# Three sets of transposes moved from TensorE to DMA in a gated attention and convolution kernel

## The chip, the cores and the metric

The kernel runs on one core of one Trainium2 chip. Times are device microseconds of one execution of the program. The profile is one such execution, with its own time; the other times are of executions without a look inside.

## The reference, cut to what matters

Two branches work on the same x of 2048 tokens by 512 features, and a gate of each token mixes them.

```
g = sigmoid((x * gate_w).sum(-1))
a = attention(x, wq, wk, wv, wo, beta)        # 32 heads of 16, 4 segments of 512 tokens
b = long_convolution(x, A, B, C, log_dt, Dskip)
return g * a + (1 - g) * b

# attention, segment by segment (phi(t) = t + 1 if t > 0 else exp(t)):
for s in range(4):
    a_dot = softmax(qs @ ks.T * scale + mask) @ vs            # causal, inside the segment
    a_mem = (phi(qs) @ M) / (phi(qs) @ z + 1e-6)              # memory of the segments before
    o     = gh * a_mem + (1 - gh) * a_dot                     # gh = sigmoid(beta), by head
    M, z  = M + phi(ks).T @ vs, z + phi(ks).sum()             # state for the next segment
out = o @ wo
```

The convolution's kernel K is a sum over 128 complex exponentials for each feature, and the convolution itself is done by a Fourier transform written as matmuls.

## The kernel before

**How work is ordered.** The kernel is first recorded as a list of operations (`Sched.op`, line 196), each with an engine, an assumed cost, the tiles it reads (`r`), writes (`w`, or `pw` for a part), and a key. `Sched.schedule` (line 268) then plays the list forward with the assumed costs. For each engine it takes the ready operation with the lowest key that could start within 0.12 us of the engine's free time, and appends it. The result is one fixed order for each engine. `Sched.emit` (line 401) writes it out with semaphore waits. On the chip each engine works strictly in that order: an operation that waits holds everything behind it. All loads, stores and copies by DMA go through one queue, SP, in the same way. The planner assumes for a DMA that SP is taken for 0.4 us, that the transfer starts 1.0 us after its issue at the earliest and after the transfer before it, that it takes bytes/215e3 us, and that it lands 1.2 us later (lines 374 to 377).

**Buffers.** Tiles come from pools of a few slots (`ek` and `rk` 2 each, `kT` 3, `o1` and `o2` 2 each, `oT` 5, `xT` 3, `xk` 1, `zs` 2). A tile is given a slot in the planned order, and the first writer waits for the last users of the slot. [...]

**Evacuations.** `S.evac` (line 256) copies PSUM to SBUF on ACT (line 258) or on DVE (line 259), as the planner chooses; line 261 is the ACT form with a scale.

**Stages.**
- Start: parameters of the convolution are loaded, turned by TensorE, and their powers are built on ACT and DVE (`ssm_prep`, `ssm_powers`), until about 60 us.
- Attention, until about 257 us: four segments, each with four head groups `hg` of 8 heads.
  - `do_xT(s)` loads 512 tokens of x by one DMA and turns them by 16 TensorE transposes into `xT[s]` (features on partitions), with two evacuations of 128x1024.
  - `gate_tokens(s)` and `seg_tokens(s)` compute the token gate and the values from `xT[s]`.
  - `project(s, hg)` makes `qT` and `kT`, 128 features by 512 tokens.
  - `seg_state(s, hg)`, for segments 0 to 2: four TensorE transposes turn `kT` to keys by token in PSUM (line 945); ACT takes their exponential (line 948), DVE their maximum with 0 (line 949) and then the minimum of the exponential with 1 (line 950); eight matmuls add phi(k) times v into the state.
  - `group(s, hg, gi)`: score tiles, exponentials of 128x1024 on ACT (line 1038), and weights times values.
  - `ophase(s, hg)`: turns the result to tokens on partitions, divides, and gets the memory part `o2` likewise. Then matmuls with the identity, accumulating over `o1` and `o2`, turn and add them in PSUM (line 1115 inside `f3`), and one evacuation makes `oT` (line 1119).
  - `oproj(s)`: the four `oT` of the segment against `wo`, stored to DRAM.
- Beside the attention run `tables(c)`, four times (DVE, lines 1169 to 1174, then 256 small matmuls and four small DMA copies), and `x_level1` (the first level of the transform of x: 16 steps, each ending in a store to DRAM).
- Tail, from about 240 us: loads of the transform's constants and results, 16 steps `K0` to `K15`, and the final mix, until 388 us.

Matmuls are recorded through the helper of line 717, so most PE work has that line.

Of the kernel before, what the change touches and what calls it, by code (L numbers as in the profile page):

```python
# [7 lines left out]
ACT = mybir.ActivationFunctionType  # L8
BF16 = mybir.dt.bfloat16
# [126 lines left out]
class Sched:  # L136
# [111 lines left out]
        self.ops.append(o)  # L248
        return o

    def dma(self, out, in_, nbytes, r=(), w=(), pw=(), key=None, slow=False, packets=0, issue=0.4):
        kw = {"allow_slow_non_contiguous": True} if slow else {}
        lat = max(nbytes / 215e3, packets * 0.0005)
        return self.op("SP", issue, lambda e: e.dma_start(out(), in_(), **kw), r=r, w=w, pw=pw, key=key, lat=lat)  # L254

# [223 lines left out]
def c_act(n):  # L479
    return 0.17 + 0.000833 * n  # L480
# [6 lines left out]
def c_tt(n):  # L487
    return 0.16 + 0.00052 * n
# [6 lines left out]
def c_ts4(n):  # L495
    return 0.15 + 0.00026 * n
# [78 lines left out]
def build_kernel(nc, A_x, A_wq, A_wk, A_wv, A_wo, A_beta, B_A_re, B_A_im, B_B_re, B_B_im,  # L575
                 B_C_re, B_C_im, B_log_dt, B_Dskip, gate_w, out):
    with contextlib.ExitStack() as es:
        S = Sched(nc, es)
        ap = S.ap
        op = S.op  # L580
        x = A_x[0]
# [17 lines left out]
        ident = cload(np.eye(128), "ident", BF16, -1)  # L599
# [30 lines left out]
        S.addr += 6 * 128  # L630
        omsP = S.pool("oms", S.addr, 512, 2)
        S.addr += 2 * 512
        A0 = S.addr
        a = A0

# [6 lines left out]
        xTP = mkpool("xT", 4096, 3)  # L642
# [16 lines left out]
        oTP = mkpool("oT", 1024, 5)  # L659
# [81 lines left out]
        xT = []  # L741

        def do_xT(s):
            S.tag = "xT"
            xks = Tile(xkP, BF16)
            S.dma(lambda: ap(xks, dims=[[512, 4], [1, 512]]),
                  lambda: bass.AP(x.tensor, x.offset + s * 4 * 128 * 512, [[512, 128], [128 * 512, 4], [1, 512]]),
                  524288, w=[xks], key=(-0.95 if s == 0 else S.key - 8))
            T = Tile(xTP, BF16)
            parts = []  # L750
            for hb in range(2):
                P = S.ps(dt=BF16)

                def f(e, P=P, hb=hb):
                    for t2 in range(2):
                        for k in range(4):
                            i = e.transpose(ap(P, t2 * 512 + k * 128, n=128), ap(xks, (2 * hb + t2) * 512 + k * 128, n=128), ap(ident, n=128))  # L757
                    return i
                op("PE", 8 * 0.07, f, r=[xks, ident], w=[P], acq=[T])
                pt = T.part()  # L760
                S.evac(lambda hb=hb, T=T: ap(T, hb * 256, [[128, 2], [512, 4], [1, 128]]), lambda P=P: ap(P, dims=[[512, 2], [128, 4], [1, 128]]),
                       1024, r=[P], pw=[pt, T], psum16=True)
                parts.append(pt)
            xT.append(T)
# [172 lines left out]
        def seg_state(s, hg):  # L937
            S.tag = "state%d" % s
            kT = proj[(s, hg)][1]
            P = S.ps(dt=BF16)  # L940
            ek, rk = Tile(ekP, BF16), Tile(rkP, BF16)

            def ft(e):
                for tb in range(4):
                    i = e.transpose(ap(P, tb * 128, n=128), ap(kT, tb * 128, n=128), ap(ident, n=128))  # L945
                return i
            op("PE", 0.27, ft, r=[kT, ident], w=[P], acq=[ek, rk])
            op("ACT", c_act(512), lambda e: e.activation(ap(ek, n=512), ap(P, n=512), ACT.Exp), r=[P], w=[ek])  # L948
            op("DVE", c_tt(512), lambda e: e.tensor_scalar_max(ap(rk, n=512), ap(P, n=512), 0.0), r=[P], w=[rk])
            op("DVE", c_ts4(512), lambda e: e.tensor_scalar_min(ap(ek, n=512), ap(ek, n=512), 1.0), w=[ek])  # L950
            hp, h2 = hg // 2, hg % 2
            if hg == 0:
                Mx[s + 1] = Tile(MxP, BF16)
            if h2 == 0:
                states[(s, hp)] = S.ps()
            PS = states[(s, hp)]

            def f(e):
                for tb in range(4):
                    for wi, T in enumerate((ek, rk)):  # L960
                        i = mm(e, ap(PS, h2 * 136, n=136), ap(T, tb * 128, n=128),
                               ap(vpad[s], tb * 544 + hg * 136, n=136), tb == 0 and wi == 0, tb == 3 and wi == 1)
                return i
            op("PE", c_mm(136, 8), f, r=[vpad[s], ek, rk], pw=[PS], acq=[Mx[s + 1]])
            if h2 == 0:
                return
            acc = lambda: ap(accT, hp * 272, n=272)
            if s == 0:
                op("DVE", c_dps(272), lambda e: e.tensor_copy(acc(), ap(PS, n=272)), r=[PS], w=[accP[hp]])
            else:  # L970
                op("DVE", c_dps(272), lambda e: e.tensor_tensor(acc(), acc(), ap(PS, n=272), ALU.add), r=[PS], w=[accP[hp]])
            op("DVE", c_f1(272), lambda e: e.tensor_tensor(ap(Mx[s + 1], hp * 272, n=272), acc(), ap(gmaskT, hp * 272, n=272), ALU.mult),
               r=[accP[hp], gmaskT], pw=[Mx[s + 1]])
# [95 lines left out]
        def ophase(s, hg):  # L1069
            S.tag = "oph%d.%d" % (s, hg)  # L1070
            ra = [raws[(s, hg, gi)] for gi in range(2)]
            P = S.ps(dt=BF16)

            def f(e):
                for tb in range(4):
                    for gi in range(2):
                        i = e.transpose(ap(P, tb * 256 + gi * 128, n=128), ap(ra[gi], tb * 128, n=128), ap(ident, n=128))  # L1077
                return i
            R1 = Tile(smP, F32)
            o1 = Tile(o1P, BF16)  # L1080
            op("PE", 8 * 0.07, f, r=ra + [ident], w=[P], acq=[R1, o1])
            op("DVE", 0.35, lambda e: e.reciprocal(ap(R1, n=32), ap(P, 16, [[256, 4], [32, 8]])), r=[P], w=[R1])  # L1082
            op("DVE", 0.2, lambda e: e.tensor_tensor(ap(R1, dims=[[8, 4], [1, 8]]), ap(R1, dims=[[8, 4], [1, 8]]),
                                                     ap(oms[s], 8 * hg, [[32, 4], [1, 8]]), ALU.mult), r=[oms[s]], w=[R1])
            op("DVE", c_dps(512), lambda e: e.tensor_tensor(ap(o1, dims=[[128, 4], [16, 8], [1, 16]]), ap(P, dims=[[256, 4], [32, 8], [1, 16]]),  # L1085
                                                            ap(R1, dims=[[8, 4], [1, 8], [0, 16]]), ALU.mult), r=[P, R1], w=[o1])
            o2 = None
            if s > 0:
                _, _, _, eq, rq = proj[(s, hg)]
                P2 = S.ps(2)  # L1090

                def f2(e):
                    for tb in range(4):
                        for wi, T in enumerate((eq, rq)):
                            i = mm(e, ap(P2, (tb // 2) * 512 + (tb % 2) * 136, n=136), ap(T, tb * 128, n=128),
                                   ap(Mx[s], hg * 136, n=136), wi == 0, wi == 1)
                    return i
                R2 = Tile(smP, F32)
                o2 = Tile(o2P, BF16)
                op("PE", c_mm(136, 8), f2, r=[eq, rq, Mx[s]], w=[P2], acq=[R2, o2])  # L1100
                op("DVE", 0.2, lambda e: e.scalar_tensor_tensor(
                    ap(R2, dims=[[16, 2], [8, 2], [1, 8]]), ap(P2, 16, [[512, 2], [136, 2], [17, 8]]), 1e-6,
                    ap(einvT, 4 * s, [[2, 2], [1, 2], [0, 8]]), ALU.add, ALU.mult), r=[P2, einvP[s]], w=[R2])
                op("DVE", 0.35, lambda e: e.reciprocal(ap(R2, n=32), ap(R2, n=32)), w=[R2])
                for hb in range(2):
                    op("DVE", c_dps(256), lambda e, hb=hb: e.tensor_tensor(  # L1106
                        ap(o2, hb * 256, [[128, 2], [16, 8], [1, 16]]), ap(P2, hb * 512, [[136, 2], [17, 8], [1, 16]]),
                        ap(R2, hb * 16, [[8, 2], [1, 8], [0, 16]]), ALU.mult), r=[P2, R2], pw=[o2])
            P3 = S.ps()
            srcs = [o1] + ([o2] if o2 is not None else [])  # L1110

            def f3(e):
                for tb in range(4):
                    for si, T in enumerate(srcs):
                        i = mm(e, ap(P3, tb * 128, n=128), ap(T, tb * 128, n=128), ap(ident, n=128), si == 0, si == len(srcs) - 1)
                return i
            oT = Tile(oTP, BF16)
            op("PE", c_mm(128, 4 * len(srcs)), f3, r=srcs + [ident], w=[P3], acq=[oT])
            S.evac(lambda: ap(oT, n=512), lambda: ap(P3, n=512), 512, r=[P3], w=[oT])
            oTs[(s, hg)] = oT  # L1120
# [280 lines left out]
```

## Time and profile before

| | us |
|---|---|
| time, median of 3 runs | 391.71 (389.81, 391.71, 398.85) |
| time of the profiled execution | 389.94 |
| its span | 388.1 |
| lines 1169, 1171 and 1174 on DVE (tables) | 35.9 + 35.6 + 34.8 busy |
| line 1038 on ACT (exponentials of scores) | 156.7 busy |
| line 258, evacuations on ACT | 89.4 busy |
| line 259, evacuations on DVE | 47.9 busy |

A group's row gives line, engine and operation, output and input, their shapes, the count, then busy time and mean ns of one, and after the last bar the idle time of that engine just before the group's instructions with what ended most of it. The granted clock of TensorE was 0.895 of full speed on average.

The page's largest waits belong to engines that had nothing else to do (ACT's evacuations for 45.1 us and DVE's for 37.5 us, both for PE); they lie for the most part in the tail, from 235 us on (40.5 and 19.2 us).

### The profile page before, as it was taken

Reading aid. Unit: us, or ns where it says so; the run is one execution under the profiler, and the core shown is the slowest. Engines: PE = TensorE matmul, PEld = TensorE weight load, DVE = VectorE, ACT = ScalarE, POOL = GpSimd, SP = SyncE. Lnnn points to the kernel's source line nnn. Section 1 sums busy time; section 2 is a strip of 40 time slices with the busy share of each in tenths; the row PEclk is TensorE's granted clock in tenths of the full one; section 3 lists DMA queues with packets and bytes.
Section 4 is the critical chain, followed back from the end, with each engine's and each line's share of the span. In section 5 each row is a group of like instructions: output and inputs, shape, how many; then the busy total and the mean of one; then the engine's idle time right before and its main releaser. Section 6 shows DMA issues by size and latency. Waiting matters only on the chain.

```text
span 388.1 us, 8595 instructions
## 1 busy us (share of the span) xinstructions
PE 326.1 (84%) x3632; PEld 146.8 (38%) x3660; DVE 290.8 (75%) x596; ACT 295.5 (76%) x383; POOL 3.2 (1%) x9
## 2 busy tenths in 40 slices
PE   4877689997998999999998999368799999999561
PEld 3323233433444435444455443233333333443120
DVE  3888897999789994999939997217638677972555
ACT  3999897999899999999989997239757679466300
POOL 1000000000000000000000000000000000000000
PEclk9985855999899999999999996759689999999768
DMA  7921000301235210000000001795227565444323
GB/s 189 270 101 56 0 2 0 110 2 56 73 112 161 83 56 30 19 3 28 28 5 19 0 2 3 122 409 157 52 69 198 168 186 156 101 120 130 81 83 162
DMA packets 25734, 34.96 MB, mean 90 GB/s; under 512 B 10976, under 2 KB 17632, under 8 KB 24800
## 3 DMA queue, kind: packets, MB, share of 16 engines
q1 hardware_dynamic: 25696, 34.41, 30.3%
q8 instruction: 29, 0.48, 0.5%
q14 instruction: 9, 0.07, 0.1%
HBM read 21.16 MB, written 8.40 MB: 76 GB/s over the span
## 4 chain that ended last, share of the span: by engine, by line
PE 45%; DVE 33%; ACT 11%; issue 5%; DMA 2%; SPq 1%; DVEq 0%
PE psum L717 44%; DVE sb L1174 6%; DVE sb L1171 6%; DVE sb L1169 6%; ACT sb L1038 6%; DVE sb L259 3%; ACT sb L258 2%; DVE sb L1306 2%; DVE sb L1085 1%; DMA sb<-in_A_wq_dram 1%; ACT sb L813 1%; SPq L254 1%; PE psum L1077 1%; DMA sb<-sb 1%; DVE sb L1106 1%
## 5 line engine op out<-in xcount | busy, mean ns | idle before, releaser
L717 PE MATMUL psum<-sb 128*32 128x20 bf16 (+16 forms) x3368 | 307.0, 276 | 46.6 <-ACT sb L1038 13.7
L717 PEld LDWEIGHTS psum<-sb 128*128 128x128 bf16 (+6 forms) x3396 | 128.2, 97 | 218.9 <-issue 90.6
L1038 ACT ACTIVATE sb<-psum 128x1024 bf16<-128x1024 f32 x160 | 156.7, 1027 | 11.3 <-PE psum L717 10.6
L258 ACT ACTIVATE sb<-psum 128x512 bf16<-128x512 f32 (+3 forms) x118 | 89.4, 778 | 51.2 <-PE psum L717 45.1
L259 DVE CAST sb<-psum 128x512 bf16<-128x512 f32 (+2 forms) x58 | 47.9, 835 | 36.5 <-PE psum L717 36.4
L1169 DVE TENSOR_TENSOR sb<-sb 128x512 bf16<-128x512 bf16 (+3 forms) x52 | 35.9, 691 | 0.6
L1174 DVE TENSOR_TENSOR sb<-sb 128x512 bf16<-128x512 bf16 (+3 forms) x52 | 34.8, 668 | 1.5
L1171 DVE TENSOR_TENSOR sb<-sb 128x512 bf16<-128x512 bf16 (+3 forms) x52 | 35.6, 685 | 0.0
L1047 DVE TENSOR_TENSOR sb<-sb 128x512 bf16<-128x512 bf16 (+1 forms) x40 | 14.3, 368 | 11.6 <-ACT sb L1038 11.6
L1306 DVE SCALAR_TENSOR_TENSOR sb<-psum,sb 128x512 bf16<-128x512 f32 x16 | 10.8, 742 | 8.4 <-PE psum L717 8.2
L1082 DVE RECIPROCAL sb<-psum 128x32 f32<-128x32 bf16 x16 | 5.7, 353 | 12.3 <-PE psum L1077 12.3
L1266 DVE TENSOR_TENSOR sb<-sb 128x1024 bf16<-128x1024 bf16 x16 | 11.0, 687 | 5.2 <-ACT sb L258 5.0
L1271 DVE TENSOR_TENSOR sb<-sb 128x512 bf16<-128x512 bf16 x32 | 13.6, 426 | 1.1
L261 ACT ACTIVATE sb<-psum,sb 128x512 bf16<-128x512 f32 x15 | 10.3, 686 | 4.8 <-PE psum L717 4.6
L1077 PE MATMUL psum<-sb 128*128 128x128 bf16 x128 | 11.5, 241 | 0.0
L1085 DVE TENSOR_TENSOR sb<-psum,sb 128x512 bf16<-128x512 bf16 x16 | 11.1, 691 | 0.5
L813 ACT ACTIVATE sb<-sb 128x1024 bf16<-128x1024 f32 x10 | 10.6, 1060 | 0.9 <-DVE sb L826 0.8
L1268 DVE TENSOR_TENSOR sb<-sb 128x1024 bf16<-128x1024 bf16 x16 | 11.0, 685 | 0.0
L1077 PEld LDWEIGHTS psum<-sb 128*128 128x128 bf16 x128 | 8.9, 108 | 3.4 <-issue 1.8
L1106 DVE TENSOR_TENSOR sb<-psum,sb 128x256 bf16<-128x256 f32 x24 | 9.1, 419 | 0.3
L757 PE MATMUL psum<-sb 128*128 128x128 bf16 x64 | 6.6, 265 | 2.9 <-DMA sb<-in_A_x_dram 1.9
L948 ACT ACTIVATE sb<-psum 128x512 bf16<-128x512 bf16 x12 | 7.1, 595 | 1.1 <-PE psum L945 1.1
(69 smaller groups left out, 135.5 us busy)
## 6 DMA issues: line engine op xcount, KB each, us to landing
sb<-c_D SPq DMA_DIRECT2D x16, 320.0 KB, 4.9
sb<-in_A_x_dram SPq DMA_DIRECT2D x8, 512.0 KB, 4.5
scr_Z<-sb SPq DMA_DIRECT2D x16, 256.0 KB, 2.1
sb<-scr_Z SPq DMA_DIRECT2D x4, 1024.0 KB, 9.1
sb<-sb SPq DMA_DIRECT2D x16, 256.0 KB
scr_abuf<-sb SPq DMA_DIRECT2D x16, 128.0 KB, 2.3
sb<-scr_abuf SPq DMA_DIRECT2D x4, 512.0 KB, 5.5
out_dram<-sb SPq DMA_DIRECT2D x4, 512.0 KB, 2.6
```

The lines of the kernel that those rows point to most:

```text
L258: fa = lambda e: e.activation(dst(), src(), ACT.Copy)
L259: fd = lambda e: e.tensor_copy(dst(), src())
L717: mm = lambda e, o_, l, r_, st, sp, **kw: e.matmul(o_, lhsT=l, rhs=r_, start=st, stop=sp, skip_group_check=True, **kw)
L813: op("ACT", c_act(1024), lambda e, pw=pw, zr=zr: e.activation(ap(pw, 0, [[512, 4], [128, 2], [1, 128]]), ap(zr, 0, [[128, 4], [0, 2], [1, ...
L1038: op("ACT", c_act(1024), lambda e, P=P, pT=pT: e.activation(ap(pT, n=1024), ap(P, n=1024), ACT.Exp, scale=0.25), r=[P], w=[pT])
L1047: op("DVE", c_tt(128 * len(offs)), lambda e, pT=pT, dims=dims: e.tensor_tensor(ap(pT, dims=dims + [[1, 128]]), ap(pT, dims=dims + [[1, 128]]),
L1077: i = e.transpose(ap(P, tb * 256 + gi * 128, n=128), ap(ra[gi], tb * 128, n=128), ap(ident, n=128))
L1085: op("DVE", c_dps(512), lambda e: e.tensor_tensor(ap(o1, dims=[[128, 4], [16, 8], [1, 16]]), ap(P, dims=[[256, 4], [32, 8], [1, 16]]), ap( ...
L1169: op("DVE", c_tt(256 * n), lambda e: e.tensor_tensor(run(tile, ne, dst, 1), run(tile, ne, src, sstep), pwv(0), ALU.mult), r=rd + [pw], w=w ...
L1171: op("DVE", c_tt(256 * n), lambda e: e.tensor_tensor(run(t2, n, 0, 1), run(tile, ne, src, sstep), pwv(1), ALU.mult), r=rd + [pw], w=[t2])
L1174: op("DVE", c_tt(256 * n), lambda e: e.tensor_tensor(D_(), D_(), ap(t2, n * 128, [[-n * 128, 2], [2 * n, 64], [1, 2 * n]]), ALU.add), r=[t ...
L1306: op("DVE", c_dps(512), lambda e, P=P, ou=ou, bl=bl, b4=b4: e.scalar_tensor_tensor(ap(ou, bl * 512, n=512), ap(P, n=512), ap(omg4T, b4, n= ...
```

## The change

Three sets of transposes become DMA transposes, issued on SP:

1. x of segments 1 to 3: for each segment, four DMAs read 512 tokens by 128 features of x from DRAM and write them turned into `xT[s]`. The load to `xk`, the 16 TensorE transposes and the two evacuations go. Segment 0 stays as it was.
2. Keys by token, segments 0 to 2: for each head group, four DMAs of 128x128 from `kT` to `rk`, in SBUF. ACT's exponential reads `rk` in place of PSUM, and DVE's maximum works on `rk` in place. The PSUM bank and four TensorE transposes go.
3. Attention output, segments 0 to 2: for each head group, DVE adds `o2` to `o1` where there is an `o2` (segments 1 and 2), and four DMAs of 128x128 turn `o1` into `oT`. The identity matmuls, the PSUM bank and the evacuation go. Segment 3 stays as it was.

The base address of the pools is also rounded up to 64 bytes. For a transpose the planner's assumed costs are those of a plain DMA. As the planner is run again, the order of all engines is new.

```diff
-    def dma(self, out, in_, nbytes, r=(), w=(), pw=(), key=None, slow=False, packets=0, issue=0.4):
+    def dma(self, out, in_, nbytes, r=(), w=(), pw=(), key=None, slow=False, packets=0, issue=0.4, tr=False):
         kw = {"allow_slow_non_contiguous": True} if slow else {}
+        if tr:
+            kw["transpose"] = True
         lat = max(nbytes / 215e3, packets * 0.0005)
...
         def do_xT(s):
             S.tag = "xT"
+            if s > 0:
+                T = Tile(xTP, BF16)
+                for k in range(4):
+                    S.dma(lambda T=T, k=k: ap(T, k * 512, n=512), lambda k=k: bass.AP(x.tensor, x.offset + s * 262144 + k * 128, [[512, 512], [1, 128]]),
+                          131072, w=(), pw=[T], key=S.key - 8, tr=True)
+                xT.append(T)
+                return
...
         def seg_state(s, hg):
             kT = proj[(s, hg)][1]
-            P = S.ps(dt=BF16)
             ek, rk = Tile(ekP, BF16), Tile(rkP, BF16)
-
-            def ft(e):
-                for tb in range(4):
-                    i = e.transpose(ap(P, tb * 128, n=128), ap(kT, tb * 128, n=128), ap(ident, n=128))
-                return i
-            op("PE", 0.27, ft, r=[kT, ident], w=[P], acq=[ek, rk])
-            op("ACT", c_act(512), lambda e: e.activation(ap(ek, n=512), ap(P, n=512), ACT.Exp), r=[P], w=[ek])
-            op("DVE", c_tt(512), lambda e: e.tensor_scalar_max(ap(rk, n=512), ap(P, n=512), 0.0), r=[P], w=[rk])
+            for tb in range(4):
+                S.dma(lambda tb=tb: ap(rk, tb * 128, n=128), lambda tb=tb: ap(kT, tb * 128, n=128), 32768, r=[kT], pw=[rk], tr=True)
+            op("ACT", c_act(512), lambda e: e.activation(ap(ek, n=512), ap(rk, n=512), ACT.Exp), r=[rk], w=[ek])
+            op("DVE", c_ts4(512), lambda e: e.tensor_scalar_max(ap(rk, n=512), ap(rk, n=512), 0.0), w=[rk])
             op("DVE", c_ts4(512), lambda e: e.tensor_scalar_min(ap(ek, n=512), ap(ek, n=512), 1.0), w=[ek])
...
+            oT = Tile(oTP, BF16)
+            if s < 3:
+                if o2 is not None:
+                    op("DVE", c_tt(512), lambda e: e.tensor_tensor(ap(o1, n=512), ap(o1, n=512), ap(o2, n=512), ALU.add), r=[o2], w=[o1])
+                for tb in range(4):
+                    S.dma(lambda tb=tb: ap(oT, tb * 128, n=128), lambda tb=tb: ap(o1, tb * 128, n=128), 32768, r=[o1], pw=[oT], tr=True)
+                oTs[(s, hg)] = oT
+                return
             P3 = S.ps()
```

## The prediction

> **What bounds the kernel now.** I read the busy times first, then the slices, then the busy times by stage, and last the chain of waits and the queue that issues the transfers.
>
> ```profile
> span 388.1 us, 8595 instructions
> PE 326.1 (84%) x3632; PEld 146.8 (38%) x3660; DVE 290.8 (75%) x596; ACT 295.5 (76%) x383; POOL 3.2 (1%) x9
> ...
> DMA  7921000301235210000000001795227565444323
> ```
>
> No engine is full over the whole span, and the transfer engines are almost idle from slice 4 to slice 23 (about 40 to 233 us), which is where the attention runs. The busy times by stage (start:end, length, then each engine with its count) say more:
>
> ```profile
> 16.00:58.00 42.00, 30.83 (x200) 12.18 (x200) 35.95 (x80) 39.42 (x60) 0.00 (x0) 0.70 0.17 55
> 58.00:96.00 38.00, 35.18 (x331) 14.34 (x334) 34.14 (x61) 34.41 (x43) 0.30 (x1) 0.88 0.13 43
> 96.00:142.00 46.00, 42.11 (x627) 20.29 (x632) 41.63 (x86) 41.78 (x56) 0.34 (x1) 0.96 0.32 102
> 142.00:172.00 30.00, 28.74 (x533) 14.86 (x537) 23.85 (x57) 28.54 (x41) 0.66 (x1) 1.00 0.06 17
> 172.00:232.00 60.00, 55.99 (x811) 28.86 (x816) 52.35 (x105) 55.43 (x76) 0.00 (x0) 1.00 0.05 13
> ```
>
> The order is PE, PEld, DVE, ACT, POOL. From 16 to 232 us (216 us) PE is busy 192.9, DVE 187.9 and ACT 199.6: all three at 87 to 92%. So this stretch is held by three engines in a fixed order, ACT fullest with 16 us of idle time. The chain of waits agrees:
>
> ```profile
> PE 45%; DVE 33%; ACT 11%; issue 5%; DMA 2%; SPq 1%; DVEq 0%
> ```
>
> It changes between engines, and only 2% of it is transfers. A late operand therefore costs nearly its full lateness, while a removed instruction gives back only what the fullest engine loses. The removed PE work has these rows (all shapes kept apart):
>
> ```profile
> L757 PE MATMUL psum<-sb 128*128 128x128 bf16 x64 | 6.6, 265 | 2.9 <-DMA sb<-in_A_x_dram 1.9 <-DVE sb L259 0.8
> L948 ACT ACTIVATE sb<-psum 128x512 bf16<-128x512 bf16 x12 | 7.1, 595 | 1.1 <-PE psum L945 1.1
> L945 PE MATMUL psum<-sb 128*128 128x128 bf16 x48 | 4.9, 227 | 1.3 <-DVE sb L259 1.0 <-DVE sb L904 0.3
> L949 DVE TENSOR_SCALAR sb<-psum 128x512 bf16<-128x512 bf16 x12 | 5.0, 416 | 0.0
> ```
>
> The nearest transfers (KB each, median us to landing) and the order of SP's first issues (start, length):
>
> ```profile
> scr_abuf<-sb SPq DMA_DIRECT2D x16, 128.0 KB, 2.3
> ...
> sb<-sb SPq DMA_DIRECT2D x16, 40.0 KB, 3.1
> ```
>
> ```profile
> 13.69 0.51 SPq L254 DMA_DIRECT2D sb<-in_B_Dskip_dram  x1
> 14.24 0.98 SPq L254 DMA_DIRECT2D sb<-in_A_x_dram  x2
> ```
>
> The new transfers take their place on SP at 14.8 us. The 40 KB row, 128 rows of 320 bytes, looks most like a transposed block of 128 rows of 256 bytes.
>
> [...] eight of line 757 at 30.38 us take 1.06 us, 0.13 each. No row shows a DMA transpose. [...] SP's plain issues here take 0.32 to 0.51 us, so my estimate is about 0.47 us an instruction. [...]
>
> **The change part by part.** A "block" is 128x128.
> 1. PE loses 6x8 transposes of x, 12x4 of keys and 80 identity matmuls of the output (segment 0: 4x4; segments 1 and 2: 8x8): 176 at 0.12 to 0.13 us, 22 us of busy time.
> 2. 18 evacuations go: 6 of 128x1024 and 12 of 128x512. The instruction order shows ACT with 12 instructions fewer and DVE with 2 more, so DVE loses 6 evacuations and gains 8 additions. ACT: 3x1.03 + 9x0.60 = 8.5 us less. DVE: 6x0.69 = 4.1 less, 8x0.43 more (row of line 1271), and the 12 maxima of line 949, now from SBUF, 0.29 for 0.42, 1.6 less: net -2.3 us. As ACT is fullest, I take **-8 us** as the most that the stretch gives back; DVE, which loses 2, could hold it to -2.
> 3. SP loses 3 plain loads and gains 108 transposes: 12 of 512x128 from x (four blocks each), 48 of key blocks, 48 of output blocks, 144 blocks in all. Its issues go from 126 to 231. At 1.31 us a block, as one stream (value taken; both ends below), that is 189 us, and some 45 plain issues of 0.4 us in the stretch add 18. They must fit between 14.8 us and the last output transpose, near 237: 222 us. The queue is 93% full.
> 4. The start. Eight transposes of x (segments 1 and 2) stand ahead of everything new: 8x5.24 = 42 us, to 57. The keys of group 0 follow, four blocks, 5.2 us, and about 2.3 us to land: 64.5 us. Those of segment 1 land at 14.8 + 21 + 2.3 = 38, but the new PE order puts segment 1's value projection right after the convolution's first matmuls on x, near 27 us, ahead of segment 0's first weights-times-values; the gate matmuls of segment 2 likewise wait to 59. Behind them stand segment 0's score tiles, so ACT gets no exponentials. ACT itself waits for the keys at 64.5, with the remaining powers and exponentials queued behind; in the trace of before its neighbours (first maximum 49.5 us, gate column sums 50.0) stand at 50. **+14.5 us**; the PE waits lie inside this, not added.
> 5. Ten later key transposes (segments 0 to 2 without the first two). The planner prices four blocks at 3x0.4 + 1.0 + 0.15 + 1.2 = 3.6 us from ready to landed; really 4x1.31 + 2.3 = 7.5, 3.9 late. The exponential waits on ACT, the maximum behind it on DVE, the state matmuls on PE, and each queues everything: 39 us, from which I take off ACT's 16 us of idle: **+23 us**. Buffers: the DMA writes into the two-slot relu buffer itself, so a transpose also waits for the state matmul two groups back, and what stands behind it on SP waits too.
> 6. Output transposes: needed only by the output projection of the whole segment, so their latency is covered; their place on SP is counted in 3. The last group's has no cover, 7.5 us against some 1.5 on PE, but at 237 us it lies beside the tail's loads: 0.
> 7. x of segment 3: 21 us of SP between output projection 0 and the keys of segment 1's group 2. PE has about 30 operations there, before's 13 to 20 us (line 261 at 122 us, line 948 at 135.5), against 21 + 7.5: **+8 us**.
> 8. Stores of the first x level and the tables' copies stand behind all this; the former's two buffers hold PE back. Inside 5. The tail after 257 us is unchanged but for slot order: 0, either sign by 2 us.
>
> Sum: -8 + 14.5 + 23 + 8 = +37.5 on the profiled run's 389.9 (span 388.1): **427 us**. The median, 391.7, is half a per cent higher; I leave that out.
>
> **Bounds of the block price.** Low: 0.47 us, the issue rate[...]. High: 2.6 us[...], an assumption, should HBM rows of 256 bytes or the plain transfers in between slow it.
>
> **The rivals.**
> A. The transposes stream at issue rate, 0.47 us. Then x lands at 14.8 + 3.8 + 4.5 (landing of the plain x load) = 23 us, before PE wants it; four key blocks take 4x0.47 + 3.1 = 5.0 us, 1.4 late, ten times 14 us, within ACT's 16 us of idle. What remains is part 2: -2 to -8, **385 us**. For it: idle transfer engines [...]. Against it: [...] that three engines at 90% leave little to absorb with. It ends on the other side of no change. It decides below about 0.7 us a block: there four key blocks take 4x0.7 + 3.1 = 5.9 us, 2.3 late, ten times 23, less 16 idle leaves 7, about what part 2 gives back.
> B. SP's stream becomes the bound. From 222/144 = 1.5 us a block (1.4 with the plain issues) it cannot finish by 237 us. At 2.6: 374 + 18 us from 14.8 on, so 407, and the tail of before from 237 to 390 behind it, part of which starts earlier: 500 to 560, **520 us**. For it: all waits of the stream are in order on one queue. [...]
> C. The request is carried out element by element. 144x16384 elements at the mean time per packet of before (30.3% of 16 x 388 us over 25696 packets, 73 ns, 16 at once) would take 11 ms; nothing speaks for it but that the trace has no such operation. 1 in 100.
>
> **How the numbers follow.** Forecast (0.8 to 1.5 us a block, 400 to 455): 0.48. A: 0.31, own range 380 to 394. B and C: 0.21. A measurement of this kernel tells about 2% from no change. Of A, 0.12 is faster than that and 0.17 within; the forecast's low end adds 0.02 within. So faster 0.12, same 0.19, slower 0.69. The range runs from 385 (0.1 left out) to 500 (0.1 left out).
>
> **What would show it.** Right: in the changed profile, SP's transposes at 14.8 us last until 50 or later; PE idle between 27 and 38 us for a transfer from x; ACT's line 953 of the new kernel waiting for a transfer several times for 3 us or more, 30 us in all; DMA in the middle slices up from 0; PE's share in the chain down and DMA's up from 2% to over 10%. Part 2 shows as ACT near 287 and PE near 304 us busy. Wrong: if the first eight transposes land before 27 us, A holds; if SP never waits for an engine after 60 us, B does.

## The result and the profile after

The changed kernel takes 405.64 us (median of 4 executions, 404.61 to 415.06), the kernel before on the same chip 393.22 (4 executions, 389.81 to 398.85): ratio 1.034, 95% interval 1.023 to 1.045, slower. Times here and below are medians of all executions, while a ratio compares the faster executions of each kernel alone, so the two can differ by up to about two per cent. The profiled execution took 406.4 us (span 404.6), 16.5 more than the profiled one of before. The direction was forecast and the time lies in the range, but the forecast cost, +37, is about three times the measured +12.4 of the medians.

The page of the changed kernel, busy times and slices:

```profile
span 404.6 us, 8431 instructions
...
PE 334.4 (83%) x3484; PEld 141.3 (35%) x3484; DVE 288.5 (71%) x598; ACT 287.2 (71%) x371; POOL 3.2 (1%) x9
...
PEclk9978555998559889999889997755759999999968
DMA  7942000101102620333222210195503956353324
```

and the one line of the page of before that the prediction did not use, the clock granted to TensorE in tenths (9 is 90% or more):

```profile
PEclk9985855999899999999999996759689999999768
```

ACT and DVE are each busy a little less than before (295.5 and 290.8). PE has fewer matmuls and is busy 8.3 us *longer* than before (326.1). The clock line goes with that: slices 10 and 11 (about 101 to 121 us) are 5s now, where before had 8 and 9, and slices 24 to 29 sum to 36 tenths where before had 41. The mean clock fell from 0.895 to 0.840. As the clock's records in the two traces (18 and 22) have full and half clock only, that is 130 us at half in place of 82. By stage, with the bounds that the prediction used:

```profile
16.00:58.00 42.00, 29.16 (x201) 11.16 (x199) 34.46 (x76) 37.88 (x58) 0.00 (x0) 0.70 0.29 63
58.00:96.00 38.00, 35.20 (x304) 13.64 (x300) 33.16 (x64) 31.93 (x38) 0.00 (x0) 0.84 0.09 18
96.00:142.00 46.00, 39.13 (x538) 17.08 (x539) 29.20 (x65) 33.61 (x46) 0.64 (x1) 0.70 0.24 61
142.00:172.00 30.00, 26.91 (x486) 12.72 (x485) 22.83 (x50) 25.79 (x34) 0.65 (x1) 0.95 0.22 63
172.00:232.00 60.00, 52.44 (x665) 23.24 (x664) 48.07 (x104) 46.16 (x65) 0.00 (x0) 0.94 0.26 74
```

The first stage, where +14.5 us were forecast, has the clock of before (0.70) and nearly its busy times. The stage from 96 to 142 us fell from 0.96 to 0.70 and does 12.4 us less DVE work and 8.2 less ACT work in the same time. The first load of the tail's constants starts at 260.6 us where it was 240.3, and the rest is 4 us shorter than before. That load's place in SP's order is new too, so it is a rough mark; and the attention does not end there, as the list of stages has it, but runs on beside the tail: its last exponential of scores (line 1038, now 1043) starts at 342.3 us, before at 327.4. The chain of waits:

```profile
PE 54%; ACT 17%; DVE 16%; issue 4%; SPq 4%; DMA 3%; DVEq 0%; ACTq 0%
```

PE's share rose from 45 to 54%, where the prediction had it fall and DMA's rise over 10%. The chain runs little over transfers, and more than before over TensorE.

**The price of a transpose.** SP's first transposes (start, length), and the transfers' rows (median us from issue to landing):

```profile
14.59 11.48 SPq L256 DMA_TRANSPOSE sb<-in_A_x_dram  x8
26.12 10.16 SPq L256 DMA_TRANSPOSE sb<-sb  x8
```

```profile
sb<-sb SPq DMA_TRANSPOSE x96, 2.4
...
sb<-in_A_x_dram SPq DMA_TRANSPOSE x12, 3.5
```

Eight transposes of x, four blocks each, take 11.48 us of SP, 1.43 each: 0.36 a block. Eight transposes of one block each take 10.16, 1.27 each. That is close to the 1.31 us a block that the prediction took, an assumption, as no trace of before has a DMA transpose; but here the price belongs to the *instruction*: one with four times the data took 13% more in these means, not four times (medians of all 12 and all 96: 1.26 and 1.23 us, the longest 2.41 and 2.46). The prediction charged 5.24 us for each of x's. (The large ones read DRAM and the small ones SBUF; no run separates the size from the source.)

**The wait that is left.** The group of ACT's exponential of the keys, then all of its waits for a transfer (total us, times, longest):

```profile
L953 ACT ACTIVATE sb<-sb 128x512 bf16<-128x512 bf16 x12 | 7.5, 626 | 13.3 <-DMA sb<-sb 13.2
```

```profile
ACT sb L953 <- DMA sb<-sb: 13.2, 3, 7.2
```

Three waits of twelve, not ten. Around the first of the long ones, ACT's timeline, then SP's and PE's (start, length, in brackets the idle time before):

```profile
90.55 2.85 ACT L1043 ACTIVATE sb<-psum 128x1024 bf16<-128x1024 f32 x3 [0.35 <-PE psum L720]
98.78 0.63 ACT L953 ACTIVATE sb<-sb 128x512 bf16<-128x512 bf16 x1 [5.38 <-DMA sb<-sb]
99.31 3.97 ACT L1043 ACTIVATE sb<-psum 128x1024 bf16<-128x1024 f32 x4
```

```profile
87.57 25.79 SPq L256 DMA_TRANSPOSE sb<-sb  x16
```

```profile
91.62 2.87 PE L720 MATMUL psum<-sb 16*128 16x384 bf16 x22 [0.36 <-ACT sb L1043]
100.37 5.72 PE L720 MATMUL psum<-sb 16*128 16x512 bf16 x40 [5.87 <-ACT sb L1043]
...
106.99 12.31 PE L720 MATMUL psum<-sb 16*128 16x256 bf16 x328
```

In SP's planned order those sixteen are four blocks of attention output of segment 0's group 2 (87.57 to 92.48), four of keys (92.53 to 97.58), four more of keys and four of output. The exponential of the first keys, which starts at 98.78, waited while the output blocks went ahead of them; nobody was in a hurry for those. Behind it on ACT stand the exponentials of the score tiles, of which the first starts at 99.31, so PE gets none and pauses for 5.87 us. In that pause, at 97.4 us, TensorE's clock falls to half, and it stays there until 121.3, although PE is busy for 20.5 of the 20.9 us from 100.4 on.

The second long wait, 7.16 us before 201.47, has four output blocks from 189.62 ahead of the keys as well. But these were wanted: they belong to the last group of segment 1, and the segment's output projection stood waiting for them:

```profile
195.76 5.14 PE L720 MATMUL psum<-sb 128*128 128x512 bf16 x26 [2.51 <-DMA sb<-sb]
```

### The profile page after: what moved, and what is told of

The parts are those of the page before. It is cut to its first block, busy times and chain, and to the rows that moved or that the text cites. A ratio compares the mean times of both kernels' runs of the same rounds, so it can differ in the third digit from the quotient of the medians.

```text
span 404.6 us, 8431 instructions
## 1 busy us (share of the span) xinstructions
PE 334.4 (83%) x3484; PEld 141.3 (35%) x3484; DVE 288.5 (71%) x598; ACT 287.2 (71%) x371; POOL 3.2 (1%) x9
## 4 chain that ended last, share of the span: by engine, by line
PE 54%; ACT 17%; DVE 16%; issue 4%; SPq 4%; DMA 3%; DVEq 0%; ACTq 0%
PE psum L720 53%; ACT sb L1043 10%; SPq L256 4%; DVE sb L261 3%; ACT sb L260 2%; DMA sb<-sb 2%; DVE sb L1318 2%; DVE sb L1186 2%; DVE sb L1183 2%; PE psum L1082 2%; DVE sb L1181 1%; DMA sb<-in_A_wq_dram 1%; ACT sb L823 1%; DVE sb L1111 1%; ACT sb L825 1%
## 5 line engine op out<-in xcount | busy, mean ns | idle before, releaser
L720 PE MATMUL psum<-sb 128*32 128x20 bf16 (+17 forms) x3316 | 322.0, 292 | 56.3 <-ACT sb L1043 21.4
L720 PEld LDWEIGHTS psum<-sb 128*32 128x32 bf16 (+6 forms) x3316 | 128.7, 100 | 245.4 <-issue 102.8
L260 ACT ACTIVATE sb<-psum 128x512 bf16<-128x512 f32 (+3 forms) x105 | 79.4, 770 | 52.8 <-PE psum L720 44.6
L261 DVE CAST sb<-psum 128x512 bf16<-128x512 f32 (+2 forms) x56 | 49.0, 880 | 44.3 <-PE psum L720 44.0
L1186 DVE TENSOR_TENSOR sb<-sb 128x512 bf16<-128x512 bf16 (+3 forms) x52 | 34.7, 668 | 1.5
L1181 DVE TENSOR_TENSOR sb<-sb 128x512 bf16<-128x512 bf16 (+3 forms) x52 | 34.6, 665 | 0.5
L1183 DVE TENSOR_TENSOR sb<-sb 128x512 bf16<-128x512 bf16 (+3 forms) x52 | 34.3, 659 | 0.0
L953 ACT ACTIVATE sb<-sb 128x512 bf16<-128x512 bf16 x12 | 7.5, 626 | 13.3 <-DMA sb<-sb 13.2
L1318 DVE SCALAR_TENSOR_TENSOR sb<-psum,sb 128x512 bf16<-128x512 f32 x16 | 10.8, 743 | 7.7 <-PE psum L720 7.5
L1082 PE MATMUL psum<-sb 128*128 128x128 bf16 x128 | 11.5, 242 | 0.2 <-DVE sb L261 0.2
L825 ACT ACTIVATE sb<-sb 128x512 bf16<-128x512 f32 x10 | 6.3, 628 | 2.2 <-DVE sb L835 2.2
```

The lines of the kernel that those rows point to most:

```text
L260: fa = lambda e: e.activation(dst(), src(), ACT.Copy)
L261: fd = lambda e: e.tensor_copy(dst(), src())
L720: mm = lambda e, o_, l, r_, st, sp, **kw: e.matmul(o_, lhsT=l, rhs=r_, start=st, stop=sp, skip_group_check=True, **kw)
L1181: op("DVE", c_tt(256 * n), lambda e: e.tensor_tensor(run(tile, ne, dst, 1), run(tile, ne, src, sstep), pwv(0), ALU.mult), r=rd + [pw], w=w ...
L1183: op("DVE", c_tt(256 * n), lambda e: e.tensor_tensor(run(t2, n, 0, 1), run(tile, ne, src, sstep), pwv(1), ALU.mult), r=rd + [pw], w=[t2])
L1186: op("DVE", c_tt(256 * n), lambda e: e.tensor_tensor(D_(), D_(), ap(t2, n * 128, [[-n * 128, 2], [2 * n, 64], [1, 2 * n]]), ALU.add), r=[t ...
```

## The experiments

The theory formed on these lines: the forecast's prices for x were wrong, key transposes are late now and then, and **the lateness costs mainly through the clock**. The rivals: the lateness itself, queue by queue, is the cost (the prediction's own theory); SP's occupation as such; and the new order of everything, since the planner is run again.

### One part at a time

In `x_alone` keys and outputs stay on TensorE, and so on:

```diff
 # keys_alone, outs_alone: x of all segments by TensorE
-            if s > 0:
+            if False:
...
 # keys_alone, x_alone: outputs of all segments by TensorE
-            if s < 3:
+            if False:
...
 # x_alone, outs_alone: seg_state as in the kernel before
```

> Only x of segments 1 to 3 is turned by DMA. Theory A (late keys: the loss is the wait of ACT for key transposes, in the profile after 13.2 us in three waits, and the half clock that TensorE pauses bring): x has 12 issues of 1.4 us, all early, so nothing waits and the time is that of before or better, 383 to 394 us. Theory B (queue: the 139 us that 108 transposes hold SP is what costs): 17 of 139 us, so within 2 us of before too. Theory C (each new plan is as good or bad as chance makes it): anywhere from 380 to 405 us, without a wait for x in the profile.

> Only the keys by token are turned by DMA (48 issues of 1.27 us). Theory A: the keys are late by themselves, four in a row take 3 x 1.27 + 2.4 = 6.2 us where the planner has 3.6, so most of the loss stays: 398 to 410 us, with ACT waiting for keys 8 us or more. Theory B: without the outputs ahead of them on SP the keys lose only the 2.6 us that the planner misses, which ACT has idle time for: 388 to 396 us, ACT waiting for keys under 4 us. Theory C: 380 to 405 us, unrelated to the waits.

> Only the attention outputs of segments 0 to 2 are turned by DMA (48 issues). Both A and B: the output projection wants them late, so within 2% of before, 384 to 398 us, unless the stores of the first x level wait behind them on SP and hold TensorE, which would show as TensorE waiting for a DMA into scr_Z. Theory C: 380 to 405 us.

| kernel | median us (executions) | ratio to before, 95% interval |
|---|---|---|
| x_alone | 397.63 (4) | 1.011, 1.001 to 1.022 |
| keys_alone | 397.65 (4) | 1.013, 0.998 to 1.027 |
| outs_alone | 397.49 (20) | 1.004, 0.998 to 1.010 |
| before, same chip | 396.43 (23) | |

No part alone shows a loss of 2%. With x alone there is no wait for x outside the load of segment 0, which before had too: parts 4 and 7 of the prediction, +22.5 us, are not there. With keys alone the exponential waits 7.0 us in 4 waits, none over 2.9: between its theories A and B, of which neither holds as stated. x_alone's time lies above the 383 to 394 us that theory A gave it. The long waits thus came with keys *and* something else on the same queue, though each of these kernels has an order of its own.

### The planner told the real price

```diff
-                          131072, w=(), pw=[T], key=S.key - 8, tr=True)
+                          131072, w=(), pw=[T], key=S.key - 8, tr=True, issue=1.42)
...
-  ... 32768, r=[kT], pw=[rk], tr=True)
+  ... 32768, r=[kT], pw=[rk], tr=True, issue=1.27)
...
-  ... 32768, r=[o1], pw=[oT], tr=True)
+  ... 32768, r=[o1], pw=[oT], tr=True, issue=1.27)
```

> All three sets as in the changed kernel, but the planner is told what an issue costs SP: 1.42 us for x and 1.27 us for the others in place of 0.4. Theory A and B: the plan puts other work before what waits for keys, so ACT's waits for keys fall from 13.2 us to under 4 and the time to 388 to 396 us. Theory C: another plan, another time, 385 to 410 us. If SP's capacity itself is short, the time stays at 400 us or more although no engine waits for a late key in the plan.

409.23 us (4 executions), ratio 1.041 (1.030 to 1.052). The waits of the exponential fell:

```profile
ACT sb L953 <- DMA sb<-sb: 5.9, 5, 2.2
```

and the time did not, so theories A and B fail. 409 us is what the expectation named for a short SP, and theory C allowed it too; fill_pauses, below, bears on both. The order is new again, so this run alone doesn't say what the cost is, only that the right price in the planner does not cure it. Its clock was 0.857, and PE paused for 3.74 us at 107 us, this time for a transfer inside SBUF.

### Keys back on TensorE, x and outputs by DMA

```diff
-            for tb in range(4):
-                S.dma(... ap(rk, tb * 128, n=128) ... ap(kT, tb * 128, n=128) ... tr=True)
...
+            def ft(e):
+                for tb in range(4):
+                    i = e.transpose(ap(P, tb * 128, n=128), ap(kT, tb * 128, n=128), ap(ident, n=128))
+                return i
```

> x and outputs by DMA, keys on TensorE as before. Lateness theory: the key waits carry the loss beyond what x and outputs cost alone (1.1% and 0.4%), so 1.5% over before. Clock theory: no 5 to 7 us wait for keys, so no long pause; clock 0.86 to 0.88 and 1 to 2% over before. If instead the sum of the issues on SP is what hurts, 60 issues (81 us of SP) cost over half of the loss: 2 to 3%.

387.04 us (7 executions, 381.96 to 394.7; before 395.12, 43 executions), ratio 0.973 (0.967 to 0.980): faster than both kernels, which none of the three theories had. It was measured a second time, on another chip:

> x of segments 1 to 3 and attention output by DMA transpose, keys by TensorE, on this chip. If it beats the kernel before: 383 to 391 us, ratio 0.965 to 0.985. Rival (the first look had a lucky set of clocks): 392 to 399 us, ratio 0.99 to 1.01.

391.50 us (6 executions, 383.85 to 398.34; before 396.82, 27 executions), between the two expectations, though within neither. With the means of all executions, the two comparisons give 0.983 +- 0.010 and 0.988 +- 0.010 (two standard errors). It is faster than before by some 1.5%; that it is over 2% isn't shown. Against the changed kernel, which stands at +3.4%, that is some 5% for the key transposes and the order that comes with them. Its PE timeline where the changed kernel paused:

```profile
93.62 6.10 PE L720 MATMUL psum<-sb 128*128 128x512 bf16 x57 [0.49 <-DVE sb L261]
```

There is no pause above 0.5 us there, and the clock is full (1.00) from 80 to 130 us.

### Pauses filled, in the same plan

The next test leaves plan and waits as they are and changes only what TensorE does in its pauses. At ten places beside pauses, useless matmuls of 128x512 are put into TensorE's order, 77 in all, at no cost to the planner, so that ACT, DVE and SP keep their order. They add zeros to a PSUM bank that is free or is being accumulated, so they change no data.

```diff
+FILL = {31: 5, 35: 7, 37: 10, 46: 8, 99: 19, 150: 5, 158: 3, 246: 10, 250: 7, 311: 3}
...
+        def filler(e, bk, n):
+            v = S.ps32[:]
+            for _ in range(n):
+                i = mm(e, bass.AP(v.tensor, v.offset + bk * 512, [[v.ap[0][0], 128], [1, 512]]), ap(ident, n=128), ap(zer, dims=[[0, 4], [1, 128]]), False, False)
+            return i
```

> The changed kernel with the same plan, and 77 useless matmuls (128x512, each adds zeros to a PSUM bank) put in front of ten TensorE operations that stood after or just before a pause in its profile: 19 of them beside the 5.9 us pause at 94.5 us, 17 at the pauses at 193 and 201 us, 30 at those from 36 to 58 us. Nothing is waited for less. Clock theory: the pauses cost more than their length because TensorE is at half clock for 24 us after the one at 94.5 and for 7 us after others; with the pauses filled the granted clock rises from 0.84 to 0.87 or more and the time falls to 388 to 398 us. Lateness theory (the waits for keys on ACT and their queues are the cost): time 403 to 412 us, at whatever clock. Plan theory (the new order is just worse): 403 to 412 us too.

397.24 us (22 executions; before 395.12), ratio 1.006 (1.002 to 1.011). Nearly all of the loss is gone, with *more* work, and with all 108 transposes still on SP: so neither a short SP nor the new order by itself holds the kernel at 3.4%. The exponential of the keys, at line 984 of this kernel, still waits:

```profile
ACT sb L984 <- DMA sb<-sb: 15.6, 5, 7.0
```

The busy times from 90 to 120 us, of the changed kernel and then with fillers:

```profile
90.00:100.00 10.00, 4.14 (x34) 1.48 (x32) 5.19 (x13) 4.27 (x6) 0.00 (x0) 0.87 0.12 23
100.00:110.00 10.00, 9.63 (x72) 3.74 (x72) 6.01 (x19) 7.03 (x10) 0.64 (x1) 0.50 0.09 19
110.00:120.00 10.00, 9.63 (x307) 4.46 (x306) 2.21 (x6) 8.00 (x11) 0.00 (x0) 0.50 0.07 13
```

```profile
90.00:100.00 10.00, 7.68 (x52) 2.77 (x51) 4.83 (x15) 4.25 (x5) 0.00 (x0) 0.82 0.09 18
100.00:110.00 10.00, 9.94 (x146) 4.36 (x138) 3.71 (x11) 6.88 (x11) 0.66 (x1) 0.67 0.11 22
110.00:120.00 10.00, 7.99 (x255) 4.78 (x252) 6.97 (x17) 8.43 (x15) 0.00 (x0) 1.00 0.19 50
```

ACT is as idle from 90 to 100 us in both (4.27 and 4.25 busy), so the wait is there. But with PE at 7.68 in place of 4.14 the clock is back at full by 110, and the 328 matmuls that took 12.31 us after the pause take 9.62:

```profile
103.86 9.62 PE L742 MATMUL psum<-sb 16*128 16x256 bf16 x328
```

The same 77 matmuls, put where PE has no pause, are the control (the diff differs in the numbers of the operations alone, and in that a group may move on by an operation if no bank is at hand):

```diff
+FILL = {64: 5, 72: 7, 81: 10, 89: 8, 178: 9, 200: 10, 218: 5, 231: 3, 265: 10, 285: 7, 300: 3}
```

> The changed kernel with the same 77 useless matmuls of 128x512, in eleven groups, but at places where TensorE of the changed kernel is busy before and after (72 to 87, 153 to 184 and 213 to 233 us), none at a pause. Theory (the useless matmuls help only by filling pauses, so that the clock stays full): the pauses and the half clock stay, lost clock 60 us or more, clock 0.84 to 0.87, and 16 us of extra busy time on top: 403 to 420 us, ratio 1.03 to 1.07. Rival (useless matmuls help anywhere, by load or by shifting the order of events): as with those at the pauses, 394 to 400 us, ratio 1.00 to 1.015.

409.47 us (6 executions), ratio 1.032 (1.026 to 1.038): as slow as the changed kernel. PE's timeline at the pause:

```profile
101.47 5.71 PE L745 MATMUL psum<-sb 16*128 16x512 bf16 x40 [4.25 <-ACT sb L1077]
...
108.08 12.31 PE L745 MATMUL psum<-sb 16*128 16x256 bf16 x328
```

The pause is there (4.25 us), and so are the 12.31 us of matmuls after it and 23.9 us of half clock. As the same number at other places gives 1.032 against 1.006, the place matters. The fillers here also take TensorE's time where it was busy, so this doesn't show that they do nothing for the clock (0.86 on average, 0.83 in the changed kernel).

Which pause matters can't be read so well. ACT and SP go through the same instructions in these three kernels, so their profiled executions can be laid side by side. With the pauses filled, ACT is 3.65 us ahead at what stood at 84.86 us in the changed kernel, 5.03 at 130.04, 6.11 at 241.66 and 10.8 at 288. The long pause and its half clock, from 85 to 130 us, thus account for 1.4 us of the 10.3; the first 85 us and the stretch from 242 to 288 gave more, 3.65 and 4.7. But the control gained 3.0 us before 60 us and 5.3 from 242 to 288 as well, with no pause filled, and lost as much in between. The gain of the ten groups together is shown, by 22 executions; what each gave is not.

### The kernel before with a pause, and with another plan

If one pause does this, it must do it to the kernel before as well. Six useless activations of 128x1024 in a row are put on ACT near 82 us:

```diff
+PAUSE = {91: 6}
...
+        def idle_act(e):
+            v = S.sb16[:]
+            return e.activation(bass.AP(v.tensor, v.offset + 104500, [[v.ap[0][0], 128], [1, 1024]]), ap(mask01, dims=[[0, 8], [1, 128]]), ACT.Copy)
```

> The kernel before with six useless activations of 128x1024 on ACT (about 6 us), near 84 us, in an otherwise unchanged order: the price of one wait of ACT as the keys caused it. Clock theory: TensorE pauses and then runs at half clock for some 20 us, so 10 to 15 us longer. Lateness theory: 6 us less what ACT's idle time takes up, so 2 to 6 us longer, without a new stretch of half clock.

407.25 us median (6 executions, 399.56 to 410.58), against 395.12. The means differ by 10.8 us, which would fit the clock theory; the ratio, 1.011 (1.004 to 1.019), says about 4, which fits the lateness theory. The profiled execution, one of the slowest at 410.58, shows the activations and the clock after them:

```profile
82.19 6.51 ACT L736 ACTIVATE sb<-sb 128x1024 bf16<-128x1024 bf16 x6
```

```profile
PEclk9985855975556999999999998757759999999967
```

Slices 9 to 12, about 92 to 133 us, stand at 5 or 6. So 6.5 us on ACT cost between 4 and 15 us, differing from execution to execution, and the executions with the lower mean clock are the longer ones (0.885 with 399.56 us, 0.839 with 410.58). That a pause can bring a long half clock to this kernel is shown by one long execution; that it does so as a rule is not.

How much another plan alone moves was measured with one constant of the planner:

```diff
-        SL = 0.12
+        SL = 0.15
```

> The kernel before with nothing changed but the planner's slack, 0.15 us in place of 0.12: the same operations in another order. Plan theory: a new order alone costs 1% or more, so the 0.4 to 1.2% of the three parts alone are nothing but that. Otherwise within 0.5% of before.

401.47 us (22 executions), ratio 1.008 (1.000 to 1.017); by the means of all executions 1.7% above before, though its mean clock was the higher one (0.888 against 0.876). A new order is thus worth up to some 2% by itself, and not through the clock. The single parts, and part of no_keys' gain, can't be told from that; the two kernels with fillers can, as they keep the changed kernel's plan.

### Fillers in kernels that have only short pauses

```diff
+FILL = {24: 7, 30: 3, 33: 8, 38: 9, 43: 4}    # in the kernel before
...
+FILL = {24: 6, 30: 5, 32: 6, 37: 9, 42: 4}    # in no_keys
```

> The kernel before, with 31 useless matmuls in five groups ahead of its own short pauses between 24 and 53 us (1.8, 0.8, 2.0, 2.2 and 1.2 us long). Theory (short pauses at half clock cost both kernels alike): lost clock falls from 41 us to 25 to 35, clock 0.91 to 0.93, gain 4 to 10 us, 386 to 391 us, ratio 0.975 to 0.99. Rival (only the pause at 94 us, which the change made, is worth filling): 393 to 400 us, ratio 0.995 to 1.01.

> x of segments 1 to 3 and attention output by DMA transpose, keys by TensorE, with 30 useless matmuls in five groups ahead of the short pauses between 25 and 52 us (1.75, 1.4, 1.6, 2.2 and 1.0 us). Theory: lost clock falls from 43 to 49 us to about 30, clock 0.91 to 0.93, 378 to 385 us, ratio 0.955 to 0.975. Rival (fillers only delay TensorE where its pauses are short): 387 to 394 us, ratio 0.98 to 1.0.

before_fill: 397.46 us (22 executions; before 396.82), ratio 1.005 (1.000 to 1.011). no_keys_fill: 391.68 us (6 executions), ratio 0.982 (0.977 to 0.988), no better than no_keys' 391.50 beside it. Both are the rival's numbers. The page of before_fill shows why nothing was gained:

```profile
PEclk9999766998559999999999996859569999999967
```

The clock is full to slice 3, as meant, but slices 10 and 11 fell to half, where before had 8 and 9. PE was idle for 2.95 us in all from 80 to 100 us (before: 2.96, the changed kernel 6.15), yet the clock was 0.82 from 90 to 100 us and 0.50 from 100 to 120 (before: 0.90, then 0.93 and 1.00). So fillers are no general gain, those in the pauses of the start gave nothing in these two kernels, and a long pause isn't the only way into the half clock.

## Why the prediction was right or wrong

**Slower: right, in part for its reason.** Keys late on ACT with all behind them were forecast and are there. The step that failed is the price of a transpose of x in parts 4 and 7, four blocks at an assumed 1.31 us, 5.24 us of SP each: it measured 1.43, and the +22.5 us that came from it are not there. Beside it, part 5 had a near number by another mechanism. Of the signs that the prediction named, ACT's 287 us and busier transfer engines came; transposes until 50 us, PE at 304, 30 us of waiting for keys and 10% of transfers in the chain did not. Term by term:

1. *PE, 22 us less busy.* Wrong as a busy time. The 176 instructions are gone (3660 weight loads before, 3484 now), yet PE is busy 8.3 us longer, with 48 us more at half clock.
2. *ACT and DVE, "-8 us".* The work was right: ACT 295.5 to 287.2 (forecast -8.5), DVE 290.8 to 288.5 (forecast -2.3). That it comes back as time shows at most in no_keys.
3. *SP.* 108 instructions take about 12 x 1.42 + 96 x 1.27 = 139 us, not 189. One block was priced well (1.31 assumed, 1.27 measured); the instruction of four blocks was not (5.24, 1.43).
4. *The start, +14.5 us.* **This term failed.** It came from eight transposes of x at 5.24 us. SP was through with them at 26.08, and group 0's keys had landed at 32.3 (forecast: 64.5); the exponential starts at 44.6 without waiting for them. Cost: none that the first stage shows.
5. *Ten late keys, +23 us.* The number is near and the mechanism is not. Three waits, 13.2 us, and filling PE's pauses brought the ratio from 1.034 to 1.006 with the waits left in. The prediction knew only waits that add up; it had no term for what a pause of PE does to the work after it. The trace records only 0.5 and 1.0 as the clock, and 2.9 us into the 5.87 us pause it fell to half. In before_fill it fell with PE idle for 2.95 us in all from 80 to 100 us, so one long pause is not the whole of it.
6. *Outputs, 0.* Right for outs_alone (1.004). Wrong beside the keys: at both long waits four output blocks, 5 us of SP, stood ahead of them. And wrong for the last group of a segment, which the prediction looked at for segment 2 alone: in segment 1 TensorE waited 2.51 us for it.
7. *x of segment 3, +8 us.* Failed as part 4 did. Its four transposes took SP from 129.37 to 134.92, 5.5 us, not 21, and nobody waited for them.
8. *The tail, 0 within 2.* Reckoned from its first load, it gave back about 4 us.

With 4 and 7 at nothing the prediction's own sum is -8 + 23 = +15, against +16.5 in the profiled executions. That this fits is partly chance, as 5 says. A second account, from the clock, fits too: over 43 executions of the kernel before in one comparison, with mean clocks of 0.853 to 0.899, the time follows 638 - 277 x clock (correlation -0.80). For the changed kernel's 0.840, just outside, this gives 405.3 us; the profiled one took 406.4. The 0.055 of clock between the two profiled executions are worth 277 x 0.055 = 15 us. A correlation alone proves no cause; that filling TensorE's pauses brings the time back is shown by fill_pauses and fill_off. How much of the loss the clock carries is not: with fillers the mean clock was 0.900, above the 0.876 of before beside it, and by the line above 0.900 would be an estimated 389 us, where 397 were measured. Some 8 us remain for the waits, the order and the useless matmuls themselves.

**The rivals.** A, transposes at issue rate (0.47 us, the author's estimate beside plain issues of 0.32 to 0.51), was near for x (0.36 us a block; the eighth landed at 27.4 us) and wrong in the time; the sign "if the first eight transposes land before 27 us, A holds" was a poor one, since it says nothing of the keys. B, SP as the bound, with an assumed 2.6 us a block, is out: SP waits for engines all through the attention (12.3 us in 10 waits for ACT's exponentials of line 1043 alone), and fill_pauses is faster with the same transposes. C is out with the first row.

**Open.** What each pause, and each late key, costs. What decides how long a half-clock stretch lasts: in before 3.4 us followed a stretch with PE busy 54% (94.7 to 98.1 us); in before_fill, with PE as busy from 90 to 100 us as in before (8.02 and 7.94 us), over 20 us of half clock did. Which part of no_keys' gain is the removed work and which the new order. A version with the keys' transposes placed ahead of the outputs' on SP was not tried.

## What to carry to other kernels

Ask what an instruction costs its queue before multiplying by its size: here a DMA transpose took 1.3 to 1.4 us of SP for one block as for four, so the 12 large ones took 17 us of the queue and the 96 small ones 122. Where TensorE is among the fullest engines, a wait that stops it may cost twice, once for the wait (here 5.87 us of pause) and once for the matmuls after it at half clock (328 of them in 12.31 us, in 9.62 with the pauses filled); look at the clock line of the page beside the busy line. And keep transfers that nobody needs soon from standing ahead of those that an engine is about to wait for.

## What the runs showed of the hardware that was not expected

- A DMA transpose of 512x128 from DRAM takes SP 1.43 us (11.48 for 8), a 128x128 one inside SBUF 1.27 (10.16 for 8); the medians over all 12 and 96 are 1.26 and 1.23. They land 3.5 and 2.4 us after issue.
- After one PE pause of 5.87 us the clock stayed at half for 23.9 us, with PE busy for 20.5 of the last 20.9; the stretches recorded in the traces of before and after are multiples of about 3.4 us, from 3.4 to 133.1. With PE kept busier in the pause, in fill_pauses (0.58 of the 3.4 us before the fall in place of 0.14) it was 10 us.
- The same program varies by 3.7% from execution to execution (388.7 to 403.3 us over 43), and the longer executions have the lower mean granted clock (correlation -0.80).
